# Instruction order from a list scheduler instead of hand-written stage offsets, in a fused linear-attention and MLP kernel

## The chip, the core and the metric

The kernel runs on one core of a Trainium2 chip. The core has five instruction queues that run beside each other, each strictly in its own order: PE (TensorE, matmuls; PEld is its weight load), DVE (VectorE), ACT (ScalarE), POOL (GpSimd) and SP (SyncE), which here issues every DMA. They wait for each other through semaphores. The metric is the device time of one execution in microseconds, here the median of three runs.

## The reference

A recurrent attention (a state of 48 x 48 per head with a decay w per step) feeds an MLP. Inputs are float32; B = 4, H = 8 heads, S = 768 steps, D = 48.

```python
for t in range(S):
    cur = np.einsum('bhd,bhe->bhde', u[None] * kt, vt)
    y[:, :, t] = np.einsum('bhd,bhde->bhe', rt, state + cur)
    state = wt[:, :, :, None] * state + np.einsum('bhd,bhe->bhde', kt, vt)
...
x = y.transpose(0, 2, 1, 3).reshape(B * S, H * D)   # 3072 x 384
h = x @ w_in                                        # 384 x 2048
r = np.maximum(h, 0.0)
out = (s * (r * r) + b) @ w_out                     # 2048 x 384
```

## The kernel before

**Attention.** The 768 steps are cut into 6 chunks of 128 for each of 4 batches: 24 chunks, numbered n so that the batch runs fastest. `load(n)` issues four DMAs on SP (w, r, k, v; rows of 48 floats). Then one chain per chunk, each step on one engine:

- `ln` (ACT): log of w. `cum` (PE): running sums of the logs by triangular matmuls, into the PSUM ring psA. `expo` (ACT): E and the chunk's decay lam.
- `mult` (DVE): prd, r and k scaled by E. `trans` (PE): eight transposes into psB. `tevac` (ACT): RK, the copy to SBUF.
- `mt` (PE): the 128 x 128 scores of each head, into psA. `mask` (DVE): mt_sb. `ymm` (PE): y from scores and old state, into psB. `yevac` (DVE): x_sb, y plus yd. `xtr` (PE) and `xevac` (ACT): the transposed xT.
- Beside it `pool1` (POOL: rkp, rku and the cast vb), `cdiag` (DVE: cd) and `pool2` (POOL: yd) make the term with u. `lam2` (POOL: l2), `dmm` (PE: d_ps) and `supd` (DVE: stmp, POOL: st) update the state for the chunk of the same batch four numbers later.

**MLP.** Two chunks make a token tile T of 256 rows; there are 12. `g1(T, i)`, i = 0 to 7, is six matmuls of 256 columns into h_ps (psH, two buffers). `relu` (ACT) writes rh, `square` (DVE) writes a part of gT. `g2(T, q)`, q = 0 to 7, is four matmuls of 384 columns into o_ps (psO, one buffer; the last tile uses psH under the name o_psh); after each four of them `oevac` (DVE) writes o_sb (four buffers), which applies s and the constant row bconst, and issues the store on SP. `colsum` makes bconst once: 16 matmuls of ones by w_out into the same psO buffer, then an ACT operation with the scalar b_bc.

**Weights.** w_in and w_out come in four pieces each, as float32 into the staging ring wst, and are cast to bfloat16 on POOL (`cast_in`, `cast_out`).

**Order.** Every step is entered as an event with a key, `at(key, fn, n)`. Keys are written by hand: chunk n starts at `base(n)` (two units apart for the first four chunks, four units after them, with a pause HOLD of 8 units), and its steps follow at fixed offsets; g1 and g2 have keys of their own (`g1key`, `g2key`), with one g1 and one g2 in each unit from the third tile on. The events are sorted by key and issued in that order; each engine gets its own instructions in this order, and all loads, the two scalar loads (`small`) and the stores share SP's queue in it. The queue begins with loads 0 and u, 1, 2, 3, four pieces of w_in, loads 4 and 5, four pieces of w_out, loads 6 and 7; later loads come at `base(n) - 22.5`.

Of the kernel before, what the change touches and what calls it, by code (L numbers as in the profile page):

```python
# [8 lines left out]
FP32 = mybir.dt.float32  # L9
BF16 = mybir.dt.bfloat16  # L10
AF = mybir.ActivationFunctionType
ALU = mybir.AluOpType
AX = mybir.AxisListType


@with_exitstack
def kernel(
# [32 lines left out]

    const = ctx.enter_context(tc.tile_pool(name="const", bufs=1))
    ain = ctx.enter_context(tc.tile_pool(name="ain", bufs=8))
    wst = ctx.enter_context(tc.tile_pool(name="wst", bufs=5))
    work = ctx.enter_context(tc.tile_pool(name="work", bufs=3))
    mlp = ctx.enter_context(tc.tile_pool(name="mlp", bufs=3))
    psA = ctx.enter_context(
# [30 lines left out]
        const.tile([128, FPP, d_model], BF16, name=f"w_out{i}", tag=f"w_out{i}")  # L87
        for i in range(NPIECE)
    ]
    NLW = 3  # L90
    logws = [
        const.tile([128, H, 64], BF16, name=f"logw{i}", tag=f"logw{i}")
# [13 lines left out]
    def coords(n):  # L106
        return n // B, n % B


    def load(n):  # L110
        cc, bb = coords(n)
        t0 = cc * L
        c = cb[n]
        c["w"] = ain.tile([128, H, D], FP32, name="wt", tag="wt")
        c["rk"] = ain.tile([128, 2, H, D], FP32, name="rkt", tag="rkt")
        c["v"] = ain.tile([128, H, D], FP32, name="vt", tag="vt")
        for src, dst in (
            (w, c["w"]),
            (r, c["rk"][:, 0]),
            (k, c["rk"][:, 1]),  # L120
            (v, c["v"]),
        ):
            nc.sync.dma_start(  # L123
                out=dst, in_=src[bb, :, t0 : t0 + L, :].transpose([1, 0, 2])
            )

    def ln(n):
        lw = logws[n % NLW]
# [3 lines left out]
    def pool1(n):  # L132
        c = cb[n]
        rkp = work.tile([128, HD], FP32, name="rkp", tag="rkp", bufs=2)
        nc.gpsimd.tensor_tensor(  # L135
            out=rkp,
            in0=c["rk"][:, 0].rearrange("t h d -> t (h d)"),
            in1=c["rk"][:, 1].rearrange("t h d -> t (h d)"),
            op=ALU.mult,
        )  # L140
        rku = work.tile([128, H, D], FP32, name="rku", tag="rku", bufs=2)
        nc.gpsimd.tensor_tensor(  # L142
            out=rku.rearrange("t h d -> t (h d)"), in0=rkp, in1=u_bc, op=ALU.mult
        )
        c["rku"] = rku
        vb = work.tile([128, H, D], BF16, name="vb", tag="vb", bufs=6)
        nc.gpsimd.tensor_copy(out=vb, in_=c["v"])
        c["vb"] = vb

    def cdiag(n):  # L150
        c = cb[n]
        cd = work.tile([128, H], FP32, name="cd", tag="cd")
        nc.vector.reduce_sum(out=cd, in_=c["rku"], axis=AX.X)  # L153
        c["cd"] = cd

    def pool2(n):
        c = cb[n]
        yd = work.tile([128, H, D], BF16, name="yd", tag="yd", bufs=4)
        nc.gpsimd.tensor_tensor(  # L159
            out=yd,  # L160
            in0=c["v"],
            in1=c["cd"].unsqueeze(2).to_broadcast([128, H, D]),
            op=ALU.mult,
        )
        c["yd"] = yd
# [46 lines left out]
    def lam2(n):  # L212
        c = cb[n]
        cc, _ = coords(n)
        if cc == NCH - 1:
            return
        l2 = work.tile([128, HP, 2], FP32, name="l2", tag="l2", bufs=4)
        nc.gpsimd.tensor_tensor(  # L218
            out=l2,
            in0=c["lam"].unsqueeze(2).to_broadcast([128, HP, 2]),  # L220
            in1=par.unsqueeze(1).to_broadcast([128, HP, 2]),
            op=ALU.mult,
        )
        c["l2"] = l2
# [94 lines left out]

    def yevac(n):  # L320
        c = cb[n]
        x = work.tile([128, HD], BF16, name="x_sb", tag="x_sb")
        nc.vector.tensor_tensor(
            out=x,
            in0=c["y_ps"][:, 0:HD],
            in1=c["yd"].rearrange("t h d -> t (h d)"),
            op=ALU.add,
        )
        c["x"] = x

    def supd(n):
        c = cb[n]
        cc, bb = coords(n)
        c["st_in"] = states[bb]
        if cc == NCH - 1:
            return
        new = work.tile(
            [128, HP, 2 * D], BF16, name=f"st{bb}", tag=f"st{bb}", bufs=2
        )
        new_v = new.rearrange("q p (g e) -> q p g e", g=2)  # L340
        lbc = c["l2"].unsqueeze(3).to_broadcast([128, HP, 2, D])
        if cc == 0:
            nc.vector.tensor_tensor(
                out=new_v,
                in0=c["d_ps"].rearrange("q p (g e) -> q p g e", g=2),
                in1=lbc,
                op=ALU.mult,
            )
        else:
            tmp = work.tile([128, HP, 2 * D], BF16, name="stmp", tag="stmp", bufs=2)  # L350
            nc.vector.tensor_tensor(  # L351
                out=tmp, in0=c["d_ps"], in1=states[bb], op=ALU.add
            )
            nc.gpsimd.tensor_tensor(  # L354
                out=new_v,
                in0=tmp.rearrange("q p (g e) -> q p g e", g=2),
                in1=lbc,
                op=ALU.mult,
            )
        states[bb] = new  # L360

    def xtr(n):
        c = cb[n]
# [12 lines left out]
    def xevac(n):  # L376
        c = cb[n]
        T, j = divmod(n, CPT)
        if j == 0:
            xT[T] = mlp.tile([128, KT, TOK], BF16, name="xT", tag="xT", bufs=3)  # L380
        nc.scalar.copy(out=xT[T][:, :, j * L : (j + 1) * L], in_=c["xt_ps"])  # L381


# [72 lines left out]
    def oevac(T, tt):  # L456
        o_sb = mlp.tile([128, d_model], FP32, name="o_sb", tag="o_sb", bufs=4)
        nc.vector.scalar_tensor_tensor(  # L458
            out=o_sb,
            in0=os_.pop((T, tt)),  # L460
            scalar=s_bc,
            in1=bconst,
            op0=ALU.mult,
            op1=ALU.add,
        )
        cc, bb = coords(T * CPT + tt)
        row0 = bb * S + cc * L
        nc.sync.dma_start(out=out[row0 : row0 + 128, :], in_=o_sb)
# [11 lines left out]
        nc.scalar.activation(out=bconst, in_=ps, func=AF.Copy, scale=b_bc)  # L480


    ev = []

    def at(key, fn, *a):
        ev.append((key, len(ev), fn, a))

    HOLD = 8

    def base(n):  # L490
        if n < B:
            return -24 + 2 * n
        return 4 * n - 16 + (HOLD if n >= B + CPT else 0)

    for n in range(N):
        q = base(n)
        at(q + 0.00, ln, n)
        at(q + 0.01, pool1, n)
        at(q + 1.20, cum, n)
        at(q + 2.00, expo, n)  # L500
        at(q + 2.01, cdiag, n)
        at(q + 3.00, mult, n)
        at(q + 3.01, lam2, n)
        at(q + 3.02, pool2, n)
        at(q + 4.20, trans, n)
        at(q + 5.00, tevac, n)
        at(q + 6.70, dmm, n)
        at(q + 7.20, mt, n)
        at(q + 7.50, supd, n)
        at(q + 8.00, mask, n)  # L510
        at(q + 9.70, ymm, n)
        at(q + 10.50, yevac, n)
        at(q + 11.50, xtr, n)
        at(q + 12.00, xevac, n)

    def g1key(T, i):
        return 1 + 8 * T + (HOLD if T >= 3 else 0) + i

    def g2key(T, i):
        if T < 2:  # L520
            return 24.6 + 4 * T + 0.5 * i
        return g1key(T + 1, 0) + i

    for T in range(NT):
        for i in range(NQ):
            q = g1key(T, i)
            at(q + 0.40, g1, T, i)
            at(q + 0.45, relu, T, i)
            at(q + 1.10, square, T, i)
        for i in range(4 * CPT):  # L530
            q = g2key(T, i)
            at(q + 0.60, g2, T, i)
            if i % 4 == 3:
                at(q + 0.70, oevac, T, i // 4)

    def cast_in(i):
        nc.gpsimd.tensor_copy(out=w_in_sb[i], in_=w_in_st[i])

    def cast_out(i):
        nc.gpsimd.tensor_copy(out=w_out_sb[i], in_=w_out_st[i])  # L540


    load(0)
    nc.sync.dma_start(
        out=u_bc, in_=u.rearrange("h d -> (h d)").partition_broadcast(128)
    )
# [10 lines left out]
    nc.vector.memset(par[0:64, 0:1], 1.0)  # L557
    nc.vector.memset(par[64:128, 1:2], 1.0)

    order = [(load, 1), (load, 2), (load, 3)]  # L560
    order += [(load_win, i) for i in range(NPIECE)]
    order += [(load, 4), (load, 5)]
    order += [(load_wout, i) for i in range(NPIECE)]
    order += [(load, 6), (load, 7)]
    for i, (fn, a) in enumerate(order):
        at(-60 + i, fn, a)
    for i in range(NPIECE):
        at(-6 + i, cast_in, i)
        at(9.05 + 2 * i, cast_out, i)
    at(16.9, colsum)  # L570

    def small():
        nc.sync.dma_start(out=s_bc, in_=moe_s.partition_broadcast(128))
        nc.sync.dma_start(out=b_bc, in_=moe_b.partition_broadcast(128))

    at(6.03, small)
    for n in range(8, N):
        at(base(n) - 22.5, load, n)

    ev.sort(key=lambda e: (e[0], e[1]))  # L580
    for _, _, fn, a in ev:
        fn(*a)


# [28 lines left out]
```

## Time and profile before

| what | value |
|---|---|
| median of 3 runs | 226.72 us (226.03 to 226.94) |
| the profiled execution | 227.96 us, its span 226.0 us |
| granted TensorE clock, mean over the span | 0.955 |
| busy share of the span: PE, DVE, POOL, ACT | 84%, 72%, 56%, 53% |
| instructions of PE, DVE, ACT, POOL | 1912, 246, 214, 150 |
| read from HBM, written | 25.36 MB, 4.72 MB |
| packets of the DMA queue under 512 B | 100656 of 107464 |

The span runs from the first to the last instruction of the core; the execution's own time is a little longer. Busy times overlap between engines. A group of instructions in the profile is named by its line, engine, output and inputs, with count, summed busy time, mean duration in ns, and the idle time of its engine ahead of it with what ended that. SPq rows are DMA issues on SP: their duration is the time the queue was held, not the transfer.

### The profile page before, as it was taken

The numbers are of one execution on the slowest core, as the hardware profiler recorded it, in microseconds if no ns is written. First come the engines' busy times: TensorE is split into PE (matmuls) and PEld (weight loads), VectorE is DVE, ScalarE is ACT, GpSimd is POOL, SyncE is SP. The second block draws the span as 40 slices with busy tenths as digits, with TensorE's granted clock in tenths as the row PEclk, the third lists the DMA queues.
The fourth block names the chain that finished last, engine by engine and source line by source line (L and its number), as shares of the span: only waits on it lengthen the run. The fifth ranks groups of instructions, "written<-read, shape, count | busy, mean of one in ns | idle before, by whom it ended". The sixth has DMA issues, their size and how long they took to land.

```text
span 226.0 us, 4923 instructions
## 1 busy us (share of the span) xinstructions
PE 189.2 (84%) x1912; PEld 141.1 (62%) x1912; DVE 163.1 (72%) x246; ACT 119.3 (53%) x214; POOL 126.2 (56%) x150
## 2 busy tenths in 40 slices
PE   1253649874919798999999999999999999999992
PEld 1142537753616555777777777777777777777761
DVE  4226944999205975799999999999999999554431
ACT  4244435763236831566676666866667666444420
POOL 2499948869008864686677767786667571000000
PEclk9999955999785999999999999999999999999999
DMA  7999989989999999668655885560100001010101
GB/s 138 192 191 259 376 161 242 376 181 198 183 164 186 189 162 231 123 122 176 148 112 125 145 172 122 121 116 35 38 35 33 7 35 38 35 38 35 39 35 71
DMA packets 107464, 30.41 MB, mean 135 GB/s; under 512 B 100656, under 2 KB 105904, under 8 KB 107440
## 3 DMA queue, kind: packets, MB, share of 16 engines
q1 hardware_dynamic: 107440, 30.09, 65.4%
q8 instruction: 15, 0.25, 0.5%
q14 instruction: 9, 0.07, 0.1%
HBM read 25.36 MB, written 4.72 MB: 133 GB/s over the span
## 4 chain that ended last, share of the span: by engine, by line
PE 70%; DVE 8%; ACT 3%; issue 2%; SPq 2%; DMA 1%; ACTq 0%
PE o_ps L448 26%; PE h_ps L415 26%; PE trps L231 4%; DVE gT L433 3%; PE mt_ps L256 3%; PE o_psh L448 2%; DVE o_sb L458 2%; PE xt_ps L366 2%; PE y_ps L293 2%; PE cums L172 2%; PE y_ps L284 1%; PE cums L175 1%; DMA b_bc<-in_moe_b_dram 1%; SPq L123 1%; ACT rh L428 1%
## 5 line engine op out<-in xcount | busy, mean ns | idle before, releaser
L428 ACT ACTIVATE rh<-h_ps 128x512 bf16<-128x512 f32 x96 | 57.3, 599 | 56.1 <-PE h_ps L415 53.4
L415 PE MATMUL h_ps<-xT,w_in 128*128 128x256 bf16 x576 | 81.6, 283 | 4.6 <-ACT rh L428 4.6
L433 DVE TENSOR_TENSOR gT<-rh 128x512 bf16<-128x512 bf16 x96 | 67.2, 705 | 24.5 <-ACT rh L428 24.2
L448 PE MATMUL o_ps<-w_out,gT 128*128 128x384 bf16 x352 | 70.9, 326 | 1.3 <-DVE o_sb L458 1.1
L415 PEld LDWEIGHTS <-w_in 128*128 128x128 bf16 x576 | 53.5, 101 | 15.1 <-issue 4.7
L448 PEld LDWEIGHTS <-gT 128*128 128x128 bf16 x384 | 36.3, 98 | 17.4 <-issue 2.0
L159 POOL TENSOR_TENSOR yd<-vt,cd 128x384 bf16<-128x384 f32 x24 | 29.2, 1215 | 5.8 <-DVE cd L153 5.7
L268 DVE TENSOR_TENSOR mt_sb<-mt_ps,tri_strict 128x1024 bf16<-128x1024 f32 x24 | 29.0, 1210 | 0.0
L135 POOL TENSOR_TENSOR rkp<-rkt 128x384 f32<-128x384 f32 x24 | 24.8, 1032 | 6.3 <-DMA rkt<-in_k_dram 6.3
L142 POOL TENSOR_TENSOR rku<-rkp,u_bc 128x384 f32<-128x384 f32 x24 | 25.9, 1080 | 3.0 <-DMA u_bc<-in_u_dram 1.2
L246 ACT COPY RK<-trps 128x1024 bf16<-128x1024 bf16 x24 | 24.2, 1007 | 2.0 <-PE trps L231 2.0
L153 DVE TENSOR_REDUCE cd<-rku 128x8 f32<-128x384 f32 x24 | 13.1, 544 | 16.4 <-POOL rku L142 16.4
L204 DVE TENSOR_TENSOR prd<-rkt,E 128x768 bf16<-128x768 f32 x24 | 24.1, 1005 | 1.1 <-ACT E L194 0.8
L354 POOL TENSOR_TENSOR st<-stmp,l 128x384 bf16<-128x384 bf16 x16 | 13.2, 828 | 18.8 <-DVE stmp L351 15.5
L172 PE MATMUL cums<-logw,tri_strict 128*128 128x384 bf16 x24 | 8.8, 368 | 16.4 <-ACT logw L130 11.9
L218 POOL TENSOR_TENSOR l<-lam,par 128x8 f32<-128x8 f32 x20 | 7.6, 379 | 26.4 <-ACT lam L198 26.3
L194 ACT ACTIVATE E<-cums 128x768 bf16<-128x768 f32 x24 | 19.4, 809 | 5.4 <-PE cums L180 5.4
L458 DVE SCALAR_TENSOR_TENSOR o_sb<-o_ps,s_bc,bconst 128x384 f32<-128x384 f32 x22 | 13.6, 618 | 11.0 <-PE o_ps L448 9.6
L381 ACT COPY xT<-xt_ps 128x384 bf16<-128x384 bf16 x24 | 11.4, 475 | 17.1 <-PE xt_ps L366 17.1
L231 PE MATMUL trps<-identity,prd 128*128 128x128 bf16 x192 | 17.1, 241 | 0.7 <-DVE prd L204 0.5
L130 ACT ACTIVATE logw<-wt 128x384 bf16<-128x384 f32 x24 | 12.7, 530 | 8.2 <-DMA wt<-in_w_dram 8.2
L231 PEld LDWEIGHTS <-prd 128*128 128x128 bf16 x192 | 14.1, 109 | 4.0 <-DVE prd L204 1.8
(45 smaller groups left out, 170.3 us busy)
## 6 DMA issues: line engine op xcount, KB each, us to landing
wt<-in_w_dram SPq DMA_DIRECT2D x24, 192.0 KB, 4.4
rkt<-in_r_dram SPq DMA_DIRECT2D x24, 192.0 KB, 4.5
rkt<-in_k_dram SPq DMA_DIRECT2D x24, 192.0 KB, 4.4
vt<-in_v_dram SPq DMA_DIRECT2D x24, 192.0 KB, 4.3
out_dram<-o_sb SPq DMA_DIRECT2D x24, 192.0 KB, 2.0
wi_st<-in_moe_w_in_dram SPq DMA_DIRECT2D x4, 768.0 KB, 8.0
wo_st<-in_moe_w_out_dram SPq DMA_DIRECT2D x4, 768.0 KB, 7.8
u_bc<-in_u_dram SPq DMA_DIRECT2D x1, 192.0 KB, 4.4
```

Of the source, the lines that this page charges most:

```text
L135: nc.gpsimd.tensor_tensor(out=rkp, in0=c["rk"][:, 0].rearrange("t h d -> t (h d)"), in1=c["rk"][:, 1].rearrange("t h d -> t (h d)"), op=AL ...
L142: nc.gpsimd.tensor_tensor(out=rku.rearrange("t h d -> t (h d)"), in0=rkp, in1=u_bc, op=ALU.mult)
L159: nc.gpsimd.tensor_tensor(out=yd, in0=c["v"], in1=c["cd"].unsqueeze(2).to_broadcast([128, H, D]), op=ALU.mult,)
L194: nc.scalar.activation(out=E, in_=ps[:, :, 0:HD], func=AF.Exp)
L204: nc.vector.tensor_tensor(out=prd[:, :, :, 0:D].rearrange("t x h d -> t (x h) d"), in0=c["rk"].rearrange("t x h d -> t (x h) d"), in1=c["E ...
L231: nc.tensor.matmul(ps[:, x * HP + p, :], lhsT=c["prd"][:, x, 2 * p : 2 * p + 2, :].rearrange("t h d -> t (h d)"), rhs=identity, is_transpo ...
L246: nc.scalar.copy(out=RK, in_=c["trps"])
L268: nc.vector.tensor_tensor(out=m.rearrange("s g p t -> s (g p) t"), in0=c["mt_ps"].rearrange("s g p t -> s (g p) t"), in1=tri_strict.unsque ...
L415: nc.tensor.matmul(ps[:, f, :], lhsT=w_in_sb[ft // FPP][:, kt, (ft % FPP) * 128 : (ft % FPP + 1) * 128], rhs=xT[T][:, kt, :], start=(f == ...
L428: nc.scalar.activation(out=rh, in_=hs[T, i], func=AF.Relu)
L433: nc.vector.tensor_tensor(out=gT[T][:, i * FPQ : (i + 1) * FPQ, :], in0=rh, in1=rh, op=ALU.mult)
L448: nc.tensor.matmul(ps, lhsT=gT[T][:, ft, tt * 128 : (tt + 1) * 128], rhs=w_out_sb[ft // FPP][:, ft % FPP, :], start=(ft == 0), stop=(ft == ...
```

## The change

All keys are removed. Each step is entered into a `Plan` with its engine, an occupancy in microseconds (`occ`), the steps it depends on (`deps`), the buffer rings it takes and the steps that release them (`takes`), and a priority. `Plan.order()` is a list scheduler: it keeps a clock per engine, and again and again picks, over all engines, the step that can start first (among equals the lowest priority number), advances that engine's clock, and appends the step. The resulting list is the order in which instructions are issued. It models:

- the end of a step as start + occ + lat (0.12 us, 0.2 for PE), and ring buffers as in the kernel;
- one shared `port` that excludes all POOL steps, DVE's `mult` and DVE's `square` from each other;
- SP as a queue in strict order of priority, with transfers of 1.03 us for a chunk's tensor and 2.15 for a weight piece, one after another; stores belong to a separate engine "SPO" of the model, though they are issued on SP as before.

Priorities put attention of chunk n at about 10 n, relu, square and oevac of tile T at 10 T, g1 at 1000 + 10 T, g2 at 2000 + 10 T + i. Beside the order, these things change: the eight weight casts move from POOL to ACT; SP's order begins loads 0 (with u after its first two tensors), 1, 2, 3, four pieces of w_in, load 4, four pieces of w_out, load 5, the two scalars, load 6 and on; ring depths wst 5 to 4, xT 3 to 6, yd 4 to 6, x_sb 3 to 4, cd 3 to 4, l2 4 to 5; `load`, `pool1`, `supd` and `oevac` are split into single steps.

```diff
+WIN_AT = 35.0
+WOUT_AT = 45.0
+CO = ('ACT', 1.3, 45.0)
+CI = ('ACT', 1.3, 20.0)
...
+    def order(self):
...
+        while any(queues.values()):
+            best = None
+            for eng, q in queues.items():
+                e = free.get(eng, 0.0)
+                pick = None
+                for o in q[: 1 if eng == "SP" else 400]:
+                    r = ready(o)
+                    if r is None:
+                        continue
+                    t = max(r, e)
+                    if o["port"]:
+                        t = max(t, port)
+                    if pick is None or t < pick[0] - 1e-9:
+                        pick = (t, o)
+                if pick and (best is None or pick[0] < best[0]):
+                    best = pick
...
+            t, o = best
+            queues[o["eng"]].remove(o)
+            free[o["eng"]] = t + o["occ"]
+            if o["port"]:
+                port = t + o["occ"]
+            fin = t + o["occ"] + o["lat"]
+            if o["dma"]:
+                dma = max(dma, t + o["occ"] + 1.0) + o["dma"]
+                fin = dma + 0.9
...
-    wst = ctx.enter_context(tc.tile_pool(name="wst", bufs=5))
+    wst = ctx.enter_context(tc.tile_pool(name="wst", bufs=4))
...
+    def cast_in(i):
+        nc.scalar.copy(out=w_in_sb[i], in_=w_in_st[i])
...
     for n in range(N):
-        q = base(n)
-        at(q + 0.00, ln, n)
-        at(q + 0.01, pool1, n)
-        at(q + 1.20, cum, n)
...
+        P = 10.0 * n
+        add(("ln", n), "ACT", 0.45, ln, (n,), [("load", n, 0)] + ([("ln", n - 1)] if n else []),
+            [("lw", [("cum", n)])], P)
...
+        add(("yd", n), "POOL", 0.8, pool2, (n,), [("cd", n), ("load", n, 3)],
+            [("yd", [("yev", n)])], P - 1, port=True)
+        add(("cum", n), "PE", 0.45, cum, (n,), [("ln", n)],
+            [("A", [("exp", n)])], P, lat=0.2)
...
+        add(("tr", n), "PE", 0.44, trans, (n,), [("mul", n)],
+            [("B", [("tev", n)])], P - 3, lat=0.2)
...
+            add(("sq", T, i), "DVE", 0.35, square, (T, i), [("relu", T, i)],
+                [], -BIG + P, port=True)
...
+                add(("store", T, tt), "SPO", 0.4, store, (T, tt), [("oev", T, tt)],
+                    [], P, dma=0.6)
+    add("colsum", "PE", 2.7, colsum, (), [("co", i) for i in range(NPIECE)] + ["small2"],
+        [("o", ["colsum"])], BIG, lat=0.8)
+    add("small", "SP", 0.1, small, (), [], [], 55.0)
+    add("small2", "SP", 0.1, small2, (), [], [], 55.1)
...
-    ev.sort(key=lambda e: (e[0], e[1]))
-    for _, _, fn, a in ev:
-        fn(*a)
+    for _, o in pl.order():
+        o["fn"](*o["args"])
```

The occupancies entered for the other steps: rkp and rku 1.0 each, vb 0.5, l2 0.17, st 0.8 (POOL); cd 0.47, mul 0.88, msk 1.14, yev 0.48, sup 0.48, oev 0.53 (DVE); exp 0.82, tev 0.92, xev 0.4, relu 0.52 (ACT); mt 0.33, ymm 0.37, xtr 0.17, dmm 0.16, g1 and g2 0.65 each (PE).

More of the change, by code (lines that the diff above doesn't have):

```diff
@@ L107, in coords, with load @@
         return n // B, n % B
-    def load(n):
+    def load(n, which):
         cc, bb = coords(n)
@@ L113, in load @@
         c = cb[n]
[L114 to L125, printed above, removed]
+        if which == 0:
+            c["w"] = ain.tile([128, H, D], FP32, name="wt", tag="wt")
+        elif which == 1:
+            c["rk"] = ain.tile([128, 2, H, D], FP32, name="rkt", tag="rkt")
+        elif which == 3:
+            c["v"] = ain.tile([128, H, D], FP32, name="vt", tag="vt")
+        src = (w, r, k, v)[which]
+        dst = c["w"] if which == 0 else c["v"] if which == 3 else c["rk"][:, which - 1]
+        nc.sync.dma_start(
+            out=dst, in_=src[bb, :, t0 : t0 + L, :].transpose([1, 0, 2])
+        )
     def ln(n):
@@ L321, in yevac @@
         c = cb[n]
-        x = work.tile([128, HD], BF16, name="x_sb", tag="x_sb")
+        x = work.tile([128, HD], BF16, name="x_sb", tag="x_sb", bufs=4)
         nc.vector.tensor_tensor(
@@ L465, in oevac, with store @@
         )
+        os_[T, tt] = o_sb
+    def store(T, tt):
+        o_sb = os_.pop((T, tt))
         cc, bb = coords(T * CPT + tt)
@@ L516, in g1key @@
[L516 to L522, printed above, removed]
+    pl = Plan(
+        dict(w=8, rk=8, v=8, lw=NLW, prd=NPR, E=2, RK=3, M=3, vb=6, yd=6, x=4,
+             cd=4, rkp=2, rku=2, l2=5, A=1, B=3, h=2, o=1, gT=3, xT=XTB, rh=4,
+             o_sb=4, wst=4, stmp=2)
+    )
+    add = pl.add
+    def cast_in(i):
+        nc.scalar.copy(out=w_in_sb[i], in_=w_in_st[i])
@@ L524 @@
+    BIG = 1000.0
     for T in range(NT):
+        P = BIG + 10 * T
         for i in range(NQ):
[L526 to L529, printed above, removed]
-        for i in range(4 * CPT):
[L531 to L546, printed above, removed]
+            add(("g1", T, i), "PE", 0.65, g1, (T, i),
+                [("xev", CPT * T + j) for j in range(CPT)]
+                + [("ci", (i * FPQ) // FPP)]
+                + ([("g1", T, i - 1)] if i else []),
+                [("h", [("relu", T, i)])]
+                + ([("gT", [("g2", T, 4 * CPT - 1)])] if i == 0 else []),
+                P, lat=0.2)
@@ new lines @@
+            add(("relu", T, i), "ACT", 0.52, relu, (T, i), [("g1", T, i)],
+                [("rh", [("sq", T, i)])], -BIG + P)
+            add(("sq", T, i), "DVE", 0.35, square, (T, i), [("relu", T, i)],
+                [], -BIG + P, port=True)
+        for i in range(4 * CPT):
+            tt, part = divmod(i, 4)
+            need = [("sq", T, ft // FPQ) for ft in range(4 * part, 4 * part + 4)]
+            if T == NT - 1:
+                need.append(("sq", T, NQ - 1))
+            need += [("co", part * 4 // FPP)]
+            if i:
+                need.append(("g2", T, i - 1))
+            take = []
+            if part == 0:
+                need.append("colsum")
+                take = [("h" if T == NT - 1 else "o", [("oev", T, tt)])]
+            add(("g2", T, i), "PE", 0.65, g2, (T, i), need, take, P + 1000 + i, lat=0.2)
+            if part == 3:
+                add(("oev", T, tt), "DVE", 0.53, oevac, (T, tt), [("g2", T, i), "colsum"],
+                    [("o_sb", [("store", T, tt)])], -BIG + P)
+                add(("store", T, tt), "SPO", 0.4, store, (T, tt), [("oev", T, tt)],
+                    [], P, dma=0.6)
@@ L558 @@
     nc.vector.memset(par[64:128, 1:2], 1.0)
[L560 to L578, printed above, removed]
-    ev.sort(key=lambda e: (e[0], e[1]))
-    for _, _, fn, a in ev:
-        fn(*a)
+    for _, o in pl.order():
+        o["fn"](*o["args"])
+    if SHOW is not None:
+        SHOW(pl)
 _INS = ['r', 'k', 'v', 'w', 'u', 'moe_w_in', 'moe_w_out', 'moe_s', 'moe_b']
```

172 lines of the change are left out of this document (138 added, 34 removed).

## The prediction, made before the change was run

> **What bounds the kernel now.** I read the stage table first (the stretches of the span, with busy time of each engine and the granted clock), then the chain that ended last, then the queue of SyncE, and the groups of instructions for prices. Columns of the stage table: length, then busy us of PE, PEld, DVE, ACT and POOL with instruction counts, then PE clock, DMA share, GB/s.
>
> ```profile
> 0.00:25.00 25.00, 9.75 (x92) 7.26 (x92) 11.59 (x22) 9.68 (x16) 17.53 (x31) 1.00 1.05 212
> 25.00:40.00 15.00, 10.51 (x108) 7.88 (x105) 8.33 (x15) 6.90 (x14) 10.96 (x11) 0.66 1.04 244
> 40.00:60.00 20.00, 14.26 (x144) 10.87 (x142) 17.68 (x22) 10.65 (x19) 13.86 (x13) 0.91 1.12 239
> 60.00:67.00 7.00, 2.56 (x24) 1.86 (x22) 0.00 (x0) 1.00 (x3) 0.00 (x0) 0.91 0.92 160
> 67.00:90.00 23.00, 20.32 (x191) 13.91 (x191) 15.68 (x24) 11.76 (x23) 15.17 (x19) 0.88 1.25 192
> 90.00:190.00 100.00, 100.00 (x1100) 76.75 (x1100) 94.07 (x136) 66.68 (x120) 68.64 (x78) 1.00 0.46 97
> 190.00:222.00 32.00, 31.78 (x269) 22.56 (x265) 15.15 (x30) 12.66 (x22) 0.00 (x0) 1.00 0.10 38
> ```
>
> From 90 to 222 us PE is never idle at full clock: an order can gain nothing there except by having less left to do. In the first 90 us PE is busy 57.4 us (the sum of five rows), so 32.6 us are idle, and what ran between 25 and 90 us ran at 0.66 to 0.91, which loses 10.51 x 0.34 + 14.26 x 0.09 + 2.56 x 0.09 + 20.32 x 0.12 = 7.5 us more. This is the whole pool the change can draw on. DVE is at 94% in the steady stretch, so there is a second bound close behind.
>
> The steady price of a chunk of 128 rows (its attention, 4 g1 and 4 g2) is read from a piece of the chain that returns every period:
>
> ```profile
> 61.88 1.01 SPq L573
> 62.93 2.99 DMA b_bc<-in_moe_b_dram
> ...
> 97.09 0.76 PE h_ps L415 x6
> ...
> 98.02 0.65 PE o_ps L448 x4
> 99.11 0.66 PE h_ps L415 x6
> ...
> 140.52 0.76 PE h_ps L415 x6
> ...
> 216.86 5.21 PE o_psh L448 x32
> 222.09 0.62 DVE o_sb L458
> ```
>
> (140.52 - 97.09) / 6 = 7.24 us of PE for each chunk. The MLP share is 4 x 0.66 + 4 x 0.65 = 5.24, so attention is 2.00. All 24 chunks need 24 x 7.24 = 173.8 us, and colsum beside them. After the last matmul (222.07) the span runs 3.9 us on. The profiled execution took 227.96 against a span of 226.0, and the median of the runs is 226.72, 0.72 above that span; I work in spans and add 0.72.
>
> **The change, part by part.**
>
> *1. The wait on b_bc.* Before, ACT stands at bconst for a 512-byte load that SyncE issues at 62.93, behind the loads of ten chunks; PE and DVE run dry from 60 to 67.
>
> ```profile
> ACT bconst L480 <- DMA b_bc<-in_moe_b_dram: 7.9, 1, 7.9
> 20.57 5.64 SPq L123 DMA_DIRECT2D rkt<-in_r_dram  x1
> ...
> 30.55 0.61 SPq L123 DMA_DIRECT2D vt<-in_v_dram  x1
> 31.20 0.81 SPq L123 DMA_DIRECT2D wt<-in_w_dram  x1
> 34.78 3.01 SPq L396 DMA_DIRECT2D wo_st<-in_moe_w_out_dram  x4
> 37.84 1.28 SPq L123 DMA_DIRECT2D wt<-in_w_dram  x1
> ...
> 48.53 0.64 SPq L123 DMA_DIRECT2D vt<-in_v_dram  x1
> 49.21 0.70 SPq L123 DMA_DIRECT2D wt<-in_w_dram  x1
> ...
> 53.09 1.10 SPq L123 DMA_DIRECT2D wt<-in_w_dram  x1
> ...
> 57.23 3.60 PE L473 MATMUL cs_ps<-w_out,ones 128*128 128x384 bf16 x16
> ```
>
> The issues themselves block while earlier transfers drain (5.64 us behind w_in). After the change the queue is loads 0 to 3 with u, w_in, load 4, w_out, load 5, the two scalars, load 6 and on. Up to load 4 it is the old order, so load 4's v still leaves at 30.55; w_out follows at 31.20 instead of 34.78, 3.58 earlier (its buffers, one fewer than before, wait for ci0 to ci3; before, the fourth cast of w_in began at 30.8, so I add nothing). Load 5 behind it takes what load 6 took, 37.84 to 49.17, shifted to 34.3 to 45.6. s_bc (1.01) and b_bc issue by 46.6 and land after 2.99: 49.6. w_out: its data move at the 35 to 46 us rates and end 3.6 earlier, about 43.5; the last cast to 45; colsum 3.60 on a cold PE, 48.7. b_bc lands last, so bconst (0.58) ends at about 50.2, and only then may g2 take the one o buffer. **T0 = 50.2**: from there I expect PE never to be out of work. Ready by then: chunks 0 to 4, g1 of tiles 0 and 1 (w_in lies there from about 31 and 16 g1 are 10.5 us), and the 16 g2 of those tiles, 10.4 us, which cover the 8 us until chunk 5 is through its chain and tile 2's g1 can start.
>
> Left at T0: 173.8 - 5 x 2.00 - 10.5 = 153.3 us. PE has been short of work before it and starts cold; the price of the last restart before stands in the row of 67 to 90: 20.32 x 0.12 = 2.4 us.
>
> 50.2 + 153.3 + 2.4 + 3.9 = 209.8 span, 210.5 as a median. The page "TensorE: Matmul & The Clock Gate" of the Trainium skill (section "What's actually happening") has the array at half clock by default and again after an idle window of about 3.4 us, released by as long a busy one. By that figure a restart costs 1.7 us, and the sum would be 209.8 as a median (an estimate from that page); the row above loses more and is used.
>
> *2. Prices for the rest.*
>
> ```profile
> L433 DVE TENSOR_TENSOR gT<-rh 128x512 bf16<-128x512 bf16 x96 | 67.2, 705 | 24.5 <-ACT rh L428 24.2
> L268 DVE TENSOR_TENSOR mt_sb<-mt_ps,tri_strict 128x1024 bf16<-128x1024 f32 x24 | 29.0, 1210 | 0.0
> L153 DVE TENSOR_REDUCE cd<-rku 128x8 f32<-128x384 f32 x24 | 13.1, 544 | 16.4 <-POOL rku L142 16.4
> L323 DVE TENSOR_TENSOR x_sb<-y_ps,yd 128x384 bf16<-128x384 f32 x24 | 13.3, 552 | 1.8 <-issue 1.0 <-PE y_ps L293 0.8
> L351 DVE TENSOR_TENSOR stmp<-d_ps,st 128x384 bf16<-128x384 f32 x16 | 8.7, 546 | 0.0
> L458 DVE SCALAR_TENSOR_TENSOR o_sb<-o_ps,s_bc,bconst 128x384 f32<-128x384 f32 x22 | 13.6, 618 | 11.0 <-PE o_ps L448 9.6
> L147 POOL CAST vb<-vt 128x384 bf16<-128x384 f32 x24 | 15.4, 640 | 0.0
> L204 DVE TENSOR_TENSOR prd<-rkt,E 128x768 bf16<-128x768 f32 x24 | 24.1, 1005 | 1.1 <-ACT E L194 0.8
> L159 POOL TENSOR_TENSOR yd<-vt,cd 128x384 bf16<-128x384 f32 x24 | 29.2, 1215 | 5.8 <-DVE cd L153 5.7
> L218 POOL TENSOR_TENSOR l<-lam,par 128x8 f32<-128x8 f32 x20 | 7.6, 379 | 26.4 <-ACT lam L198 26.3
> L537 POOL CAST w_in<-wi_st 128x1536 bf16<-128x1536 f32 x4 | 5.7, 1462 | 1.8 <-DMA wi_st<-in_moe_w_in_dram 1.8
> L246 ACT COPY RK<-trps 128x1024 bf16<-128x1024 bf16 x24 | 24.2, 1007 | 2.0 <-PE trps L231 2.0
> L381 ACT COPY xT<-xt_ps 128x384 bf16<-128x384 bf16 x24 | 11.4, 475 | 17.1 <-PE xt_ps L366 17.1
> ```
>
> *3. Eight casts go from POOL to ACT.* No row has a 1536-wide cast on ACT. At least 1.01 (the 1024-wide copy), at most 4 x 0.475 = 1.90; the line through both copies gives 1.007 + 512 x 0.83 ns = 1.43, and I take it as nearest: 11.4 us over ACT, which goes from 119 to 131 of some 214 us. ACT is busy 17.6 of the 35 us from 25 to 60, so it hides them; uncovered is only the last cast before colsum, counted above, and a wrong price moves it by 0.5 us, inside the 0.9 us until b_bc. POOL loses 8 casts, which nothing waited on late in the span; what they held up on DVE lies before T0. Nothing for both.
>
> *4. DVE and POOL in the stretch after T0.* The scheduler puts attention first, so chunks run ahead of the MLP (xT now has 6 buffers). It makes its POOL operations and DVE's prd and squares exclude each other: POOL 4.27 us per chunk, prd 0.88, squares 4 x 0.35 per chunk of MLP. A chunk then takes p with p = 5.15 + 1.4 (p - 2.00) / 5.24, so p = 6.3 us, and MLP advances 0.82 chunk in it. These are the diff's own numbers and I use them only for the mixture. By the rows DVE needs for it: cd 0.54, prd 1.005, mask 1.21, x 0.55, state 0.55 = 3.86, and 0.82 x (4 x 0.705 + 0.62) = 2.82; 6.68 in 6.3, 0.38 over. For the 18 chunks after load 5 that is 6.8 us if squares stay at 705 ns as now, and nothing if the order avoids the collisions (no gain: PE is the bound there already). Between the ends I take the middle, **3.4**, as the group mixes squares of about 0.42 with long ones.
>
> *5. Stores on SyncE.* The scheduler gives stores a queue of their own, but they are issued on the queue of the loads, at the place of the planned time. It counts 0.6 us an issue and no blocking; about loads 6 to 12 stand ahead of the first store. By 49.21 to 53.09 and on, a chunk's loads take 4 to 4.2 us of queue, so that store leaves at about 46.6 + 7 x 4.15 = 75.7 and frees its o_sb near 78. The fifth oevac needs it, and every square and mask behind it on DVE. PE reaches that point after 5 halves of g2 (13 us), 8 or 16 g1 and four chunks of attention (8): 50.2 + 26 to 31 + 2.4 = 78.6 to 83.6. So 0 us is likely; the far end is a fifth oevac at 71 (g1 of tile 3 and two chunks late), 7 us. I take **1**.
>
> *6. Free edits.* Split helpers (pool1, supd, load) issue the same instructions. The deeper rings (xT, yd, x, cd, l2) only remove waits. psA stays single: cum, exp, mt, mask on it make about 3.4 us per chunk, under 6.3. At the end g1 is ahead, so tile 10's g2 would expose o_sb gaps (0.63 each on the chain); tile 11 uses the other PSUM ring and can fill them: 0, at most 4 x 0.7 = 2.8.
>
> Sum: 210.5 + 3.4 + 1 = **215 us**, 5% under 226.72.
>
> **The rivals.**
>
> *A. Everything hides.* b_bc lands with less queue ahead (bound by colsum, 48.7, so 1.5 less), with a cold start of half the price and no collision: 210.5 down to 207. For it: PE had no idle time at all from 90 to 190 under DVE at 94%. Against: item 4.
>
> *B. The order has no slack, and PE waits: slower.* The scheduler places a PE step the moment its own model has the input ready; PE then stands still, in order, if reality is later. Its prices are below the rows for yd (0.80 against 1.215), vb (0.50 against 0.64), l2 (0.17 against 0.379) and the square (0.35 against 0.705): 1.12 us per chunk. If each of the 19 chunks from 5 on hands that to PE, 21.3 us, 210.5 + 21.3 = 231.8. It decides against the change from 16.2 / 19 = 0.85 us per chunk on. For it: these durations swing with what the other engine does.
>
> ```profile
> L159 POOL TENSOR_TENSOR yd<-vt,cd x24: 823/1271/1572, 13.9 to 188.2; 128x384 bf16<-128x384 f32 x24
> L433 DVE TENSOR_TENSOR gT<-rh x96: 408/476/1678, 36.0 to 217.4; 128x512 bf16<-128x512 bf16 x96
> ```
>
> Against: the gap between 0.42 and 1.68 is mostly waiting, and the scheduler counts that wait apart, by its exclusion. The page "SBUF — State Buffer" of the Trainium skill (section "Who interferes with whom") says that a DVE instruction with two SBUF inputs and a GpSimd one that reads SBUF exclude each other, and that the order of issue decides which is held; so a swapped pair holds the other engine for a whole instruction. The minimum and maximum above (0.82 and 1.57) fit that rule.
>
> *C. Stores hold DVE* at more than one oevac: 210.5 + 3.4 + 7 = 221.
>
> *D. No change:* the earlier start is given back in the stretch after T0, 226 to 228.
>
> **How the numbers follow.** My case (210.5 to 220) 0.59, A 0.15, B 0.14, C 0.06, D 0.06. Faster by over 0.5% are mine, A and C, 0.80; D is within 0.5% (about what this measurement can tell from no change); B slower, 0.14. The range drops B and the edge of A, and reaches to the other cases: 207 to 227.
>
> **What would show it.** bconst ends near 50 and PE is at nine tenths or more from there to the end: item 1. Squares well under 705 ns: A; near it, with DVE at 95% or more and PE at 95% between 60 and 160: item 4. A first store issued after 70 us with oevac waiting for a DMA: items 5 and C. PE idle in short pieces before trps, mt and xtr in every chunk: B. The forecast is wrong if T0 is later than 55, or PE loses over 10 us after it.

## The result and the profile after

The changed kernel takes 219.25 us (median of 4 executions, 217.68 to 219.93) against 226.83 beside it: a ratio of 0.966 (95% interval 0.960 to 0.972), 7.6 us less. The profiled execution, the longest of the four, took 219.93 with a span of 218.2. Of run a6 below, five of the ten executions, the profiled one among them, were some 2% longer at a lower granted clock; its ratio is that of the other five, and its trace is not read for times. Forecast were 215 us, with a range of 207 to 227.

The stage table of the changed kernel comes first (columns as before: length, busy us of PE, PEld, DVE, ACT, POOL, then clock, DMA share and GB/s), cut at the start of the first g2 and at the end of attention's rush:

```profile
0.00:51.20 51.20, 32.78 (x308) 24.15 (x309) 28.94 (x51) 34.54 (x52) 25.52 (x39) 1.00 0.98 227
51.20:66.00 14.80, 12.36 (x140) 8.58 (x140) 10.20 (x15) 8.68 (x18) 11.83 (x16) 1.00 1.24 186
66.00:160.00 94.00, 89.12 (x1044) 67.72 (x1042) 88.34 (x130) 65.36 (x119) 69.23 (x81) 1.00 0.78 143
160.00:213.10 53.10, 52.88 (x423) 37.81 (x421) 24.37 (x51) 20.14 (x35) 7.07 (x8) 1.00 0.12 42
```

The same cut of the kernel before:

```profile
0.00:51.20 51.20, 28.77 (x306) 22.31 (x307) 31.00 (x50) 24.45 (x43) 37.00 (x49) 0.90 1.03 235
51.20:66.00 14.80, 8.32 (x59) 5.56 (x56) 6.60 (x8) 2.77 (x6) 5.35 (x5) 0.88 1.13 179
66.00:160.00 94.00, 90.32 (x964) 67.87 (x964) 81.02 (x118) 58.90 (x110) 65.08 (x77) 0.97 0.78 142
```

PE is idle 18.4 us up to 51.2 (before: 22.4) and 2.4 up to 66 (6.5), and from 51 us on no row shows a low clock any more. From 66 to 160 it is idle 4.9 us where it was idle 3.7: behind the start the new order does worse, and before, those 3.7 all lay ahead of 90. That is the shape of the result: a gain at the start, part of it given back in the middle. What PE waited for after 51 us, with total, count and longest:

```profile
PE xt_ps L465 <- DVE x_sb L417: 1.7, 2, 1.0
PE cums L266 <- ACT logw L217: 1.5, 2, 0.9
PE trps L325 <- DVE prd L298: 1.4, 3, 1.0
PE cums L266 <- ACT lam L292: 0.9, 1, 0.9
PE y_ps L387 <- DVE mt_sb L362: 0.8, 1, 0.8
PE mt_ps L350 <- DVE mt_sb L362: 0.8, 1, 0.8
PE o_ps L547 <- ACT bconst L583: 0.4, 1, 0.4
PE d_ps L403 <- POOL l L312: 0.2, 1, 0.2
```

These are many waits of at most 1 us, nearly all of an attention step for the engine ahead of it. The wait for b_bc has shrunk from 7.9 us to 0.6 (first row, out of all waits; second and third, SyncE's queue):

```profile
ACT bconst L583 <- DMA b_bc<-in_moe_b_dram: 0.6, 1, 0.6
...
47.75 0.43 SPq L603 DMA_DIRECT2D b_bc<-in_moe_b_dram  x1
...
82.83 1.29 SPq L571 DMA_DIRECT2D out_dram<-o_sb  x1
```

### The profile page after: what moved, and what is told of

Same layout as the page of the kernel before. It is cut to its first block, busy times and chain, and to the rows that moved or that the text cites. A ratio compares the mean times of both kernels' runs of the same rounds, so it can differ in the third digit from the quotient of the medians.

```text
span 218.2 us, 4916 instructions
## 1 busy us (share of the span) xinstructions
PE 187.7 (86%) x1912; PEld 138.4 (63%) x1912; DVE 153.1 (70%) x246; ACT 128.7 (59%) x222; POOL 113.7 (52%) x142
## 4 chain that ended last, share of the span: by engine, by line
PE 50%; DVE 22%; SPq 7%; DMA 6%; issue 6%; ACT 5%; POOL 2%; DVEq 0%; ACTq 0%; POOLq 0%
PE h_ps L514 19%; PE o_ps L547 16%; DVE gT L532 7%; SPq L210 6%; DVE prd L298 5%; DVE mt_sb L362 4%; DMA rkt<-in_k_dram 4%; PE trps L325 4%; DVE o_sb L557 3%; PE mt_ps L350 2%; DMA wt<-in_w_dram 2%; PE o_psh L547 2%; PE y_ps L387 1%; ACT RK L340 1%; DVE x_sb L417 1%
## 5 line engine op out<-in xcount | busy, mean ns | idle before, releaser
L514 PE MATMUL h_ps<-xT,w_in 128*128 128x256 bf16 x576 | 78.7, 277 | 2.5 <-ACT rh L527 2.4
L527 ACT ACTIVATE rh<-h_ps 128x512 bf16<-128x512 f32 x96 | 57.4, 613 | 31.5 <-PE h_ps L514 30.5
L547 PE MATMUL o_ps<-w_out,gT 128*128 128x384 bf16 x352 | 70.1, 326 | 0.6 <-ACT bconst L583 0.4
L532 DVE TENSOR_TENSOR gT<-rh 128x512 bf16<-128x512 bf16 x96 | 52.8, 570 | 24.0 <-ACT rh L527 23.9
L253 POOL TENSOR_TENSOR yd<-vt,cd 128x384 bf16<-128x384 f32 x24 | 22.8, 949 | 21.8 <-DVE cd L247 21.7
L298 DVE TENSOR_TENSOR prd<-rkt,E 128x768 bf16<-128x768 f32 x24 | 27.1, 1130 | 6.1 <-DMA rkt<-in_k_dram 4.5
L233 POOL TENSOR_TENSOR rku<-rkp,u_bc 128x384 f32<-128x384 f32 x24 | 27.4, 1143 | 0.3
L454 POOL TENSOR_TENSOR st<-stmp,l 128x384 bf16<-128x384 bf16 x16 | 15.4, 964 | 9.2 <-DVE stmp L445 9.1
L417 DVE TENSOR_TENSOR x_sb<-y_ps,yd 128x384 bf16<-128x384 f32 x24 | 13.2, 549 | 7.4 <-PE y_ps L387 5.0
L325 PEld LDWEIGHTS <-prd 128*128 128x128 bf16 x192 | 12.8, 105 | 8.8 <-DVE prd L298 7.9
L241 POOL CAST vb<-vt 128x384 bf16<-128x384 f32 x24 | 15.8, 659 | 0.0
```

The costliest lines, as they stand in the source:

```text
L233: nc.gpsimd.tensor_tensor(out=rku.rearrange("t h d -> t (h d)"), in0=c["rkp"], in1=u_bc, op=ALU.mult)
L253: nc.gpsimd.tensor_tensor(out=yd, in0=c["v"], in1=c["cd"].unsqueeze(2).to_broadcast([128, H, D]), op=ALU.mult,)
L298: nc.vector.tensor_tensor(out=prd[:, :, :, 0:D].rearrange("t x h d -> t (x h) d"), in0=c["rk"].rearrange("t x h d -> t (x h) d"), in1=c["E ...
L325: nc.tensor.matmul(ps[:, x * HP + p, :], lhsT=c["prd"][:, x, 2 * p : 2 * p + 2, :].rearrange("t h d -> t (h d)"), rhs=identity, is_transpo ...
L514: nc.tensor.matmul(ps[:, f, :], lhsT=w_in_sb[ft // FPP][:, kt, (ft % FPP) * 128 : (ft % FPP + 1) * 128], rhs=xT[T][:, kt, :], start=(f == ...
L527: nc.scalar.activation(out=rh, in_=hs[T, i], func=AF.Relu)
```

## The experiments

Ratios are against the kernel before, run on the same chip beside each, with 95% intervals.

### 1. How much of the gain is one small load

Theory G1: what held the kernel before was bconst waiting for b_bc. G2: it was the order as a whole. The first run moves only the two scalar loads in the old kernel.

```diff
-    at(6.03, small)
+    order += [(lambda _: small(), 0)]      # behind load 5 and the last w_out piece
     order += [(load, 6), (load, 7)]
```

> The kernel before with one edit: the two scalar loads stand behind the last w_out piece and load 5 on SyncE, as early as in the changed kernel, instead of behind load 9. Theory G1 (a good part of the gain is the wait of bconst for b_bc): PE's 4.4 us idle between 60 and 67 us go and some of the slow clock after it, 226.8 to 221-222. Theory G2 (the gain is the scheduler's order; without it another load is late next): 225-227.

220.94 us, 0.976 (0.971 to 0.981): 5.5 us less, as G1 says. The edit does not bring an early g2: b1's first one starts at 71.7 us (77.7 in the kernel before, 51.2 in the changed one), and bconst now waits for colsum. What it removes is the wait of 4.6 us that PE had in one piece at 62.6 us, and the slow clock behind it. The mirror moves them back in the changed kernel, with nothing else in the order altered:

```diff
-    add("small", "SP", 0.1, small, (), [], [], 55.0)
-    add("small2", "SP", 0.1, small2, (), [], [], 55.1)
+    add("small", "SP", 0.1, small, (), [], [], 95.0)
+    add("small2", "SP", 0.1, small2, (), [], [], 95.1)
```

> The changed kernel, same order, with the two scalar loads behind load 9 on SyncE instead of load 5 (the mirror of b1). G1 (the early scalars carry the start): b_bc lands near 68 instead of 50.5 us, ACT and PE stand behind bconst, 230-236. G2 (something else keeps g2 from starting): 219-222.

236.09 us, 1.041 (1.039 to 1.044). Its waits:

```profile
ACT bconst L583 <- DMA b_bc<-in_moe_b_dram: 15.4, 1, 15.4
PE o_ps L547 <- ACT bconst L583: 15.2, 1, 15.2
```

Two small loads behind the wrong neighbours cost 16.8 us over the changed kernel, more than the whole change brings. G1 holds both ways. Against b1 the changed kernel, with all its parts, is 1.7 us ahead by the times and about 2.3 by the ratios, and the two intervals (0.960 to 0.972 and 0.971 to 0.981) touch: a small gain, hardly shown.

Then everything of the change but the scheduler: SyncE's new order, casts on ACT, ring depths, on the hand-written offsets.

```diff
-    order += [(load, 4), (load, 5)]
+    order += [(load, 4)]
     order += [(load_wout, i) for i in range(NPIECE)]
+    order += [(load, 5)]
+    order += [(lambda _: small(), 0)]
...
-        nc.gpsimd.tensor_copy(out=w_in_sb[i], in_=w_in_st[i])
+        nc.scalar.copy(out=w_in_sb[i], in_=w_in_st[i])
```

> The kernel before with everything of the change except the scheduler's order: SyncE's order of loads (w_out ahead of load 5, scalars behind it), casts on ACT, the ring depths; the hand-written offsets stay. G1: 219-222, most of the 7.6 us without any scheduler. G2: 224 or more.

229.08 us, 1.013 (1.009 to 1.017). This lies in G2's range, and G1's forecast for it was a miss. It is 8 us slower than b1, which has the early scalars too, so the parts beside the order are a loss under the old one. PE's waits in b3, and in b1 below it:

```profile
PE cums L172 <- ACT logw L130: 20.6, 5, 6.5
```

```profile
PE cums L172 <- ACT logw L130: 12.1, 4, 4.5
```

Cum stands early in the hand-written order, with g1 queued behind it, and two of its waits make the difference. Four rows of b3 (casts and ln on ACT, cum of chunks 4 and 5 on PE), then cum of chunk 4 in b1:

```profile
32.54 5.59 ACT L537 CAST w_in<-wi_st 128x1536 bf16<-128x1536 f32 x4
38.03 0.52 ACT L130 ACTIVATE logw<-wt 128x384 bf16<-128x384 f32 x1
38.60 0.48 PE L172 MATMUL cums<-logw,tri_strict 128*128 128x384 bf16 x1 [6.48 <-ACT logw L130]
47.65 0.32 PE L172 MATMUL cums<-logw,tri_strict 128*128 128x384 bf16 x1 [3.21 <-ACT logw L130]
```

```profile
33.25 0.48 PE L172 MATMUL cums<-logw,tri_strict 128*128 128x384 bf16 x1 [0.99 <-ACT logw L130]
```

For chunk 4, ln stands on ACT behind four casts that POOL had before: 6.5 us of wait instead of 1.0. For chunk 5, cum waits 3.2 us, since load 5 now comes behind w_out. So the changed kernel is about 2 us ahead of the best hand order here, and the scheduler's list 10 us ahead of the same parts in the old order. No run parts b3's three parts; by these rows the casts on ACT cost the most, which is the opposite of what section 4 shows under the scheduler's list.

### 2. What PE waits for in the middle

My prediction had put it on DVE. T1: DVE, with collisions on the port it shares with POOL, paces attention. T2: steps are placed without slack and drift late. First DVE is relieved, then POOL, the order unchanged:

```diff
-        nc.vector.reduce_sum(out=cd, in_=c["rku"], axis=AX.X)
+        nc.vector.reduce_sum(out=cd, in_=c["rku"][:, :, 0:6], axis=AX.X)
```

> The changed kernel with cd summed over 6 of 48 columns (it leaves out the rest of the sum), same order: about 0.35 us less DVE per chunk, in an operation that does not touch POOL's port. T1 (after the start DVE with its collisions paces attention and PE waits in order): up to 18 x 0.35 = 6 us less, 213-215, and mask of chunk 23 starts 5 us earlier. T2 (PE waits because the steps are placed without slack on a latency, DVE's load is not it): 218-219.5.

217.24 us, 0.959 (0.955 to 0.964). DVE's busy time fell by 6 us, the kernel's by 2, which lies between the two forecasts.

```diff
     def pool1(n):
-        rkp = work.tile(...); nc.gpsimd.tensor_tensor(out=rkp, ...)
+        pass
...
-            out=rku..., in0=c["rkp"], in1=u_bc, op=ALU.mult
+            out=rku, in0=c["rk"][:, 0], in1=c["rk"][:, 1], op=ALU.mult
```

> The changed kernel with the product by u left out (rku = r*k in one POOL operation instead of two), same order: POOL has 1.05 us less per chunk, DVE the same instructions. T1 with collisions as the cause: squares under 570 ns and prd under 1130 ns in the mean, 2 to 4 us less, 215-217.5. If collisions are not it: squares as now and 218.5-219.5. T2: 218-219.5.

217.63 us, 0.961 (0.958 to 0.965), again between the forecasts. Both intervals overlap the changed kernel's, so each gain is at most suggested. Squares and prd, first in the changed kernel and then in a2, did not get shorter when POOL had less to do:

```profile
L532 DVE TENSOR_TENSOR gT<-rh 128x512 bf16<-128x512 bf16 x96 | 52.8, 570 | 24.0 <-ACT rh L527 23.9
L298 DVE TENSOR_TENSOR prd<-rkt,E 128x768 bf16<-128x768 f32 x24 | 27.1, 1130 | 6.1 <-DMA rkt<-in_k_dram 4.5 <-ACT E L288 1.6
```

```profile
L525 DVE TENSOR_TENSOR gT<-rh 128x512 bf16<-128x512 bf16 x96 | 52.8, 570 | 24.1 <-ACT rh L520 23.8
L291 DVE TENSOR_TENSOR prd<-rkt,E 128x768 bf16<-128x768 f32 x24 | 27.3, 1139 | 7.4 <-DMA rkt<-in_k_dram 3.9 <-ACT E L281 3.4
```

The rows of 66 to 160, a1 and then a2:

```profile
66.00:160.00 94.00, 89.90 (x1057) 68.46 (x1055) 85.52 (x133) 65.07 (x118) 69.71 (x81) 1.00 0.75 142
```

```profile
66.00:160.00 94.00, 89.02 (x1051) 67.54 (x1049) 88.10 (x132) 64.70 (x117) 53.25 (x66) 1.00 0.76 142
```

PE's idle time there is 4.1 and 5.0 us, against 4.9: with DVE down to 91%, or POOL down by 16 us in this stretch, PE waits almost as long. (In a7 of section 4, where PE has the changed kernel's order once more, it is idle 5.0 us there, and 1.4 instead of 2.4 from 51 to 66: so a microsecond in the start says little.) T1 fails as the main cause. T2 is tried by giving each attention step a margin in the scheduler's model:

```diff
+    for o in pl.ops.values():
+        if o["name"][0] in ("ln", "mul", "tev", "msk", "yev"):
+            o["lat"] += 0.6
     for _, o in pl.order():
```

> The changed kernel whose scheduler counts 0.6 us more between an attention step on DVE or ACT (ln, mult, tevac, mask, yevac) and the PE step behind it: the same work with a margin. U2: the lag of mask behind the scheduler's plan grows by 3-4 us after the start instead of 7.1, 216-217.5. U1: lag smaller at most by what the plan itself gets longer, 218.5-221.

222.33 us, 0.981 (0.977 to 0.985): slower than the changed kernel by 3 us, beyond what either theory expected. The lag of mask behind the plan grows from chunk 5 to chunk 23 by 7.3 us, as without the margin (7.1), so T2's own sign does not come. But the loss lies ahead of that stretch:

```profile
0.00:51.20 51.20, 30.26 (x274) 21.99 (x275) 26.11 (x46) 32.69 (x47) 25.00 (x39) 0.93 1.02 234
```

PE is idle 20.9 us here instead of 18.4, the clock falls to 0.50 between 40 and 45 us, and the first g2 starts at 52.5. From there to 160 us PE is idle 6.2 us instead of 7.3. So the run shows that this margin costs at the start, and does not rule out that one behind the start would help. The other idea is the mixture: PE spends g1 first, by priority, and g2 comes after all g1. U1: with the two kinds mixed, as the hand-written order has them, PE always finds one that is ready.

```diff
-            add(("g2", T, i), "PE", 0.65, g2, (T, i), need, take, P + 1000 + i, lat=0.2)
+            add(("g2", T, i), "PE", 0.65, g2, (T, i), need, take, P + i, lat=0.2)
```

> The changed kernel with one number: g2 of a tile has the priority of g1 of the same tile (P + i) instead of coming after all g1 (P + 1000 + i), so that the scheduler mixes the two. U1 (the 7.7 us that PE stands still after the start come from an order that spends g1 first, waits on the two h buffers and has no g2 left beside attention): PE idle after 51 us falls to 2-4 us, 213-216. U2 (they come from steps placed without slack that drift late): idle as now, 218-219.5.

216.63 us, 0.957 (0.953 to 0.960). Its table:

```profile
51.20:66.00 14.80, 13.84 (x163) 9.74 (x162) 12.79 (x17) 9.36 (x18) 13.23 (x16) 1.00 1.18 181
66.00:160.00 94.00, 90.32 (x1045) 67.14 (x1044) 89.65 (x128) 63.30 (x114) 70.08 (x82) 1.00 0.76 143
```

Idle 1.0 and 3.7 us, 4.6 in place of 7.3: time and idle time moved as U1 says, and both stopped just short of its ranges; the interval touches that of the changed kernel. The scheduler's own clocks have the same gain: by `Plan.order()` PE is idle 5.3 us behind the first g2 in the changed kernel and 1.9 in a3, so a good part of these waits stands in the plan itself. Both edits together:

> Both edits (margin 0.4). U1 alone: as a3 or up to 2 us slower, since the margin costs at the start. U1 and U2 together: 1-3 us faster than a3.

218.66 us, 0.964 (0.961 to 0.968), 2 us slower than a3, as U1 alone had it. The first g2 starts only at 53.1 us, for 49.8 in a3; from 66 to 160 us PE is idle 2.5 us, the least of all runs here:

```profile
66.00:160.00 94.00, 91.50 (x1071) 69.15 (x1071) 90.58 (x130) 65.50 (x119) 70.36 (x82) 1.00 0.81 144
```

A margin on all chunks, the first ones too, does not pay with either mixture.

### 3. Loads that come later than planned

By the scheduler's plan k of load 5 lands at 44.4 us; POOL, which waits for it, starts at 49.03, and at 53.76 for load 6 (plan 48.5). The three rows are chunks 4, 5 and 6:

```profile
34.77 0.99 POOL L222 TENSOR_TENSOR rkp<-rkt 128x384 f32<-128x384 f32 x1 [6.33 <-DMA rkt<-in_k_dram]
49.03 1.00 POOL L222 TENSOR_TENSOR rkp<-rkt 128x384 f32<-128x384 f32 x1 [6.52 <-DMA rkt<-in_k_dram]
53.76 1.00 POOL L222 TENSOR_TENSOR rkp<-rkt 128x384 f32<-128x384 f32 x1 [0.83 <-DMA rkt<-in_k_dram]
```

With honest transfers in the model, alone and then with a3's priority:

```diff
-                dma = max(dma, t + o["occ"] + 1.0) + o["dma"]
+                dma = max(dma, t + o["occ"] + 2.5) + o["dma"]
...        # dma=1.03 -> 1.06 for a tensor, 2.15 -> 2.6 for a weight piece
```

> The changed kernel with only the later transfers in the scheduler's model. Loads later than planned as a cause: PE idle from 51 to 66 us from 2.5 to under 1 us, 217-218.5. Otherwise 219-220.5.

222.16 us, 0.982 (0.977 to 0.987): 3 us slower than the changed kernel, a miss. The rows say how far the theory goes:

```profile
51.20:66.00 14.80, 14.54 (x168) 10.57 (x167) 11.95 (x17) 9.89 (x20) 12.39 (x16) 1.00 1.22 182
66.00:160.00 94.00, 86.73 (x999) 64.84 (x997) 90.50 (x126) 63.14 (x116) 64.44 (x78) 1.00 0.77 140
```

From 51 to 66 us the idle time is 0.3 us instead of 2.4 (1.4 in a7), but up to 51.2 it is 19.3 instead of 18.4, and the first g2 starts at 52.3: a part of the wait has only moved ahead. From 66 to 160 it is 7.3 instead of 4.9, and DVE is at 96%: the list that follows from the other start happens to be a worse one. With the mixed priority:

> a3 (g2 with g1's priority) with the scheduler's transfers as late as they were measured in the changed kernel (2.5 us to the start of a transfer instead of 1.0, 1.06 us for a tensor, 2.6 for a weight piece): k of load 5 at 50.2 in the plan against 49.0 measured and 44.4 planned so far. If the waits of PE up to 66 us come from loads that are later than planned: 1-2 us less than a3, 214.5-215.5. If not: 216-217.5.

216.50 us, 0.955 (0.954 to 0.957); idle 0.3 and 3.3 us. It is the fastest of all here, clearly ahead of both kernels, and not told apart from a3. By its own expectation this is the case "if not": up to 66 us PE is idle 19.5 us in all, and 19.2 in a3, so the gap of 51 to 66 us went and came back ahead of it.

### 4. The casts

> The changed kernel with the eight weight casts on POOL, as before, 1.4 us each and on the shared port in the scheduler's model too. My item 3 priced the move at nothing: 218.5-220.5. If ACT is what keeps POOL and DVE free for attention at the start: g2 starts 2-3 us later, 221-223.

The ratio is 1.004 (1.000 to 1.007), so about 227 us, 7 to 8 us slower than the changed kernel and beyond both forecasts. Here the scheduler was told of the casts on POOL (1.4 us each, on the shared port), and its whole list is another. In a7 the list is that of the changed kernel and only the engine of the casts differs:

```diff
     def cast_in(i):
-        nc.scalar.copy(out=w_in_sb[i], in_=w_in_st[i])
+        nc.gpsimd.tensor_copy(out=w_in_sb[i], in_=w_in_st[i])
```

> The changed kernel, the same order on every other engine, with the eight casts issued on POOL instead of ACT at their places. It parts the two readings of a6. If POOL's time and its port are the price of casts there: a6's loss stays, 225 or more. If a6 lost by the order that the scheduler made of it (colsum on PE behind the transposes of chunk 5, which wait for load 5; g2 at 57.5 instead of 51.2 us): 219-221.5, colsum at 46-49 us.

218.4 us, 0.964 (0.959 to 0.968): as the changed kernel, and a little under the forecast. The casts' rows, ACT in the changed kernel and POOL in a7:

```profile
L597 ACT CAST w_out<-wo_st 128x1536 bf16<-128x1536 f32 x4 | 6.5, 1615 | 0.0
L594 ACT CAST w_in<-wi_st 128x1536 bf16<-128x1536 f32 x4 | 5.9, 1477 | 0.0
```

```profile
L597 POOL CAST w_out<-wo_st 128x1536 bf16<-128x1536 f32 x4 | 6.8, 1722 | 1.9 <-DMA wo_st<-in_moe_w_out_dram 1.9
L594 POOL CAST w_in<-wi_st 128x1536 bf16<-128x1536 f32 x4 | 5.8, 1466 | 0.0
```

So under this list the engine is worth nothing, and the loss of a6 is in the order made for it. Where in the order is open: in a6's list colsum does stand on PE behind the transposes of chunk 5, as the expectation has it, but no run moves that step alone.

## Why the prediction was right, and by which steps short

The sign, the range and the first mechanism were right; 215 was 4 us too low. In spans, 214.2 was forecast and 218.2 measured. By the prediction's own terms, from the table above:

| term | forecast | measured | difference |
|---|---|---|---|
| T0, start of g2 | 50.2 | 51.2 | +1.0 |
| PE work after T0 | 153.3 | 155.0 (12.36 + 89.12 + 52.88 + 0.60 in the rest) | +1.7 |
| cold restart | 2.4 | 0 | -2.4 |
| waits after T0 | 4.4 (items 4 and 5) | 7.5 (2.4 + 4.9 + 0.2) | +3.1 |
| end | 3.9 | 4.5 (last matmul 213.7) | +0.6 |

The work done by T0 was the forecast's (16 g1 and the attention of chunks 0 to 4, with cum of chunk 5), so the 1.7 us more of PE work lie in its price after T0; no run shows where. The errors cancel in part: without the restart that was never paid, the forecast would have been 6.4 us too low.

**Item 1** held, with one part off. b_bc issued at 47.75 for the forecast 46.6, and bconst started at 50.56. But b_bc does not land clearly last: ACT, without an idle piece from 31.5 to 50 us, ended the last cast at 49.6 for the forecast 45, and colsum ended at 50.4 for 48.7, just as b_bc landed. In a1 and a7, where b_bc was earlier, bconst waits for colsum, and the first g2 starts at 50.0 and 49.8. That T0 came out within 1 us is in part luck. a10 shows by itself that the early scalars are needed for T0. What I did not see is that the old order with this one edit comes within about 2 us, with its first g2 at 71.7: I compared the change with the kernel before only, and took T0 for the measure of the gain.

**The cold restart** failed: the granted clock is 1.00 in the rows after T0. In this order no PE wait near T0 is long (the longest after 28 us is 1.2 us), where before it stood 4.6 us in one piece. In a10, with a wait of 15.2 us, the clock of 51 to 66 us is 0.55:

```profile
51.20:66.00 14.80, 0.38 (x2) 0.21 (x2) 0.00 (x0) 1.01 (x3) 1.07 (x2) 0.55 1.34 183
```

So the rule of the Trainium skill that the prediction weighed (page "TensorE: Matmul & The Clock Gate", section "What's actually happening": half clock after an idle window of about 3.4 us) agrees with both kernels and with a10, though no run here measures the limit. My term should have asked how long the gap is.

**Item 4** was the step that failed, in cause and size. I priced DVE's overload at 0 to 6.8 us and took 3.4. Squares fell from 705 to 570 ns in the mean (631 in a7, which has the same order) while prd rose from 1005 to 1130, and DVE is at 94% between 66 and 160. A chunk of attention took 5.75 us, from the mask of chunk 5 to that of chunk 23, where the item's sum had 6.3. Yet a1 takes 6 us off DVE and a2 16 off POOL, and PE's idle time in that stretch moves by 0.8 us at most. Most of the 4.9 us stand there for another reason. A part stands in the plan itself: a3 removes 1.2 of them by priority alone. What the remaining 3.3 to 3.7 us of a3 and a8 wait for in common is not settled; with the margin of a5 it is 2.5.

**Item 5** and rival C: the first store left at 82.83, later still than the forecast 75.7, and no oevac waited for one: 0, not 1.

**Item 3** was right in a7. But "nothing" holds for the engine alone, and only under this list, as b3 shows: there the casts held up ln on ACT. And a6, a4 and a9 show that a small change of a model's number, fed through the scheduler, can make the kernel 3 to 8 us slower.

**Rival B** had the place right and the price wrong: mask of chunk 5 starts at 58.4 us, 4.5 behind the plan, that of chunk 23 at 161.9, 11.6 behind, 0.40 us per chunk where it needed 0.85. Part of that lag is no wait: a chunk takes 7.24 us of PE and the plan counts 7.12. And the cure that B suggests, a margin, made it slower, by what it costs at the start.

**Rival A** came in one part only: the cold start cost nothing. Squares got shorter, but PE's idle time stayed.

## What to carry to other kernels

Before crediting a rewrite of an order with a gain, try the old order with its single longest wait removed: here two small loads, moved ahead of four chunks, brought 5.5 of the 7.6 us. A more honest model does not by itself give a better list: correcting transfer times that were 5 us early made the kernel 3 us slower alone and no faster on top of a3's priority, so each corrected list has to be timed. Look at the scheduler's own planned idle time before blaming lateness: the priority that kept one kind of PE work back cost 3.4 us by the plan and 2.6 on the chip. A step that costs nothing under one order can cost much under another, as the casts on ACT did.

## What the hardware showed that I had not expected

The cast of 128 x 1536 from float32 takes 1.48 us on ACT and 1.47 on POOL (w_in), and 1.6 and 1.7 for w_out: little reason to prefer one by speed. SyncE's issue of a 192 KB load behind four 768 KB pieces held the queue for 6.44 us in the changed kernel, where a free one takes 0.4:

```profile
22.00 6.44 SPq L210 DMA_DIRECT2D rkt<-in_r_dram  x1
28.48 3.55 SPq L210 DMA_DIRECT2D rkt<-in_k_dram  x1
```

A scheduler that counts 0.6 us for the issue of a tensor is wrong there by a factor of ten, and this is where its transfers begin to run ahead of the real ones: k of this load lands at 31.7 us by the plan, and POOL, which waits for it, starts at 34.77.

The clock column reads 1.00 over the first 25 us of both kernels, and the matmuls there do not bear it out. The first one of cum in the changed kernel, for chunks 3 and 4:

```profile
21.53 0.52 PE L266 MATMUL cums<-logw,tri_strict 128*128 128x384 bf16 x1
37.23 0.33 PE L266 MATMUL cums<-logw,tri_strict 128*128 128x384 bf16 x1
```

By such rows PE is slow until about 31 us in the changed kernel; in the kernel before it is slow up to 24 us and again from 28 to 38. So the pool of 7.5 us that the prediction counted from 25 us on left out the start, and a clock column is best read beside the duration of one instruction that returns.
